# mLSTM cell and exact-GELU block on one Trainium2 core: the decays' turning split in two, and the front's steps in a new order

## Chip, cores and metric

The kernel runs on one core of one Trainium2 chip. The metric is the device time of one execution in microseconds (us), the median of several runs. The engines are TensorE (PE, with its weight loads as PEld), VectorE (DVE), ScalarE (ACT), GpSimd (POOL) and SyncE (SP), which issues all DMAs here.

## The reference

An mLSTM cell runs over a sequence, and its output goes through a block of two matrices with an exact GELU between them.

```
batch, heads, seq, head_dim = 4, 8, 768, 40
for t in range(seq):
    m_new = max(f[t] + m, i[t])
    f_stab, i_stab = exp(f[t] + m - m_new), exp(i[t] - m_new);  m = m_new
    C = f_stab * C + i_stab * outer(v[t], k[t])
    n = f_stab * n + i_stab * k[t]
    y[t] = sigmoid(o[t]) * (C @ q[t]) / max(|n . q[t]|, 1)
x = y as (3072 tokens, 320);  out = gelu(x @ w_in) @ w_out      # w_in 320 x 2048, w_out 2048 x 320
```

Everything is float32; the two weight matrices arrive as float64, and the kernel converts their bits itself.

## The kernel before

**Chunks.** The sequence is cut into six chunks of 128 steps. Within a chunk the cell is a masked product of 128 by 128 per head (queries by keys, times weights that come from the gates), and a state of 40 by 41 per head carries over to the next chunk. A unit of work is one chunk c of one batch entry b: eight heads. A chunk of all four entries makes 512 tokens, which then go through the GELU block.

**The front.** The program first does the cell for chunks 0 and 1 and the whole GELU block for chunk 0, mixed with the conversion of all 26 weight pieces. This stage is the front. It takes up the first 133 us of the profiled execution. After it, the function `up` and the string DOWN handle each further chunk in the same way; neither is touched.

**The order is written by hand.** The string FRONT is a list of words. `play` goes through it and calls one step for each word; the letter names the step and the digits are its arguments. Every step issues its instructions on the engines' queues at once, and each engine works through its queue in that order, waiting for its inputs and for free buffers. So the place of a word sets the place of all its instructions on PE, DVE, ACT, POOL and SP. DMAs are issued by SP, also in order, and each waits until the one eight places before it has landed.

The steps that the texts speak of (small letters for chunk 0, capitals for chunk 1, the digit is the batch entry):

- `E`, `N` (`second_gates`, `later_gates`): the gate scans on DVE, the write of M to DRAM (`M_d`), the turns of `a` on PE into `aT`, and the exponentials of `ew` and `gg` on ACT. For chunk 0 they run ahead of the list.
- `Q`, `D` (`decays_turned`, L242): turn `ew` and `gg` on PE (L216), copy them to `ewT` and `gT` on DVE (L217), then spread the last row of `gT` over all partitions with a product (`pd`, L246) and copy it to `dec` (L248). Q is for the later chunks, D for the first.
- `w`/`W` (`weights`): for chunk 0, five-part products on PE into two PSUM banks `pm` (L394, L396), then eight exponentials on ACT (L399); for chunk 1 the input is a row broadcast from `M_d` by a DMA (`B`, L160), masked on POOL (`M`, L373).
- `t`/`T` (`turn`): keys and queries turned on PE (`pt`, L442), copied as `kT`, `qT` by ACT (L445). `s`/`S` (`scores`): 16 passes on PE (`ps`, L468) and two products with the weights on DVE (L471).
- `c`/`C` (`carry`): the state's products (`pf`, L487, L492); for chunk 0 it first weighs the values on DVE (`vw`, L455). `v`/`V` (`values`): `ph`, L531.
- `g`, `y`, `x`: the output gate's sigmoid on ACT (L405); the finishing on DVE (L544 to L549) with a small copy `y_rest` (L555); the turn to tokens (`px`, L566). For chunk 1 `X` is followed by `R` (`split_x`).
- `P`, `L`, `O`, `B`: DMAs only (weight pieces; q and k; v and output gate; the broadcast of `M_d`). `L0` and `O0` belong to batch entry 0 of chunk 0, `L4` and `O4` to entry 0 of chunk 1.
- `K`, `J` (`conv_one`, `conv_two`): the next weight piece's two conversion steps: three DVE instructions and two on ACT, then two on DVE (L337, L340) and the DMA of the piece four places on.
- `A`, `U`: up steps (`pu`, L671, L677, then GELU on ACT, L681) for the two halves of chunk 0's tokens. `F`: one row of the down product (`po`, L779). `Z`: one weight tile split in two parts.
- `k` (`warm`, L198): n products that nobody reads ("cold"). `I` (`keep_clock`): as many unread products (L354) ahead of the next step that allows for them.

Each word of the kind K, J, A, U, F or Z takes the next item of its own list, so only its place matters.

Of the kernel before, what the change touches and what calls it, by code (L numbers as in the profile page):

```python
# [25 lines left out]


FRONT = """
    k3 O0 L0 g0 I2 I2 E P0 w0 t0 P1 L1 k5 N k1 O2 P2 L3 L2 w1 K Q D s0 O1 t1 w2 c0 P3 K v0 I1 J K s1 y0 I4 I3 w3 t2
    I6 O3 v1 g1 L4 J I2 c1 I2 I3 K y1 s2 x0 t3 O4 B5 x1 J L5 B4 s3 v2 g3 g2 c2 v3 y2 T0 H G0 c3 K J x2 O6 y3 O5 A x3  # L30
    J M1 K K J M0 W0 L6 A J M2 W1 S0 C0 T1 K J U U K K T2 V0 A O7 J W2 G1 K M3 J K S1 C1 G2 Y0 L7 A W3 S2 V1 J J Y1
    C2 K T3 J K U U J S3 V2 K C3 K J K J J F K F F J F K X0 J G3 K J K V3 F F F J R0 K Y2 Z J F K K F J F K X1 J F R1
    F J K F X2 F B8 F Y3 J Z X3 R2 B9 R3 B10 F"""
DOWN = """
    M0 Z M1 W0 F L3 F W1 Z Z F S0 Z S1 K2 C0 M2 Z C1 G0 G1 G2 G3 V0 Z V1 W2 Z M3 F Q2 K3 Q3 Y0 D3 F F W3 F Z S2 S3
    C2 C3 V2 V3 F N F Y1 X0 R0 Y2 F F Y3 X1 R1 F X2 R2 F X3 R3 F"""
# [3 lines left out]
def kernel(  # L40
# [18 lines left out]
    B, H, S, D = q.shape  # L59
    L = P  # L60
    NCH = S // L
# [67 lines left out]
    def load(n, first=0, end=4):  # L129

        if n >= NCH * B:
            return
        c, b = divmod(n, B)
        for src, dst in ((q, qb), (k, kb), (v, vb), (o_gate, None))[first:end]:
            nc.sync.dma_start(out=dst[turn_of(n)][:, :, 0:D] if dst else out_of(n),
                              in_=src[b, :, c * L:(c + 1) * L, :].rearrange("h p d -> p h d"))
# [73 lines left out]
    def gates_turned(*parts):  # L210

        for src, dst in parts:
            n = dst.shape[1]
            pg = ps_tr.tile([P, n, BH], F32, name="pg", tag="tr")
            for c in range(n):
                nc.tensor.transpose(pg[:, c, :], src[:, c, :], ident[0:BH, 0:BH])  # L216
            nc.vector.tensor_copy(out=dst, in_=pg)  # L217
# [24 lines left out]
    def decays_turned(e0, e1, g0, g1):  # L242
        e, g = slice(e0, e1), slice(g0, g1)
        gates_turned((ew[:, e], ewT[:, e]), (gg[:, g], gT[:, g]))
        pd = ps_tr.tile([P, g1 - g0, BH], F32, name="pd", tag="tr")
        nc.tensor.matmul(pd.rearrange("p c n -> p (c n)"), last, gT[:, g].rearrange("p c n -> p (c n)"),  # L246
                         start=True, stop=True)
        nc.vector.tensor_copy(out=dec[:, g], in_=pd)  # L248
# [65 lines left out]
    def conv_one(i):  # L314

        if i < len(pieces):
            n = bits[i].shape[1]
            lo, hi = bits[i][:, :, 0], bits[i][:, :, 1]
            s = sig[i] = raw.tile([P, WP], F32, name="sig", tag="sig")[:, 0:n]
            p = pow2[i] = raw.tile([P, WP], F32, name="pow", tag="pow")[:, 0:n]  # L320
            su, pu = s.bitcast(U32), p.bitcast(U32)

            nc.vector.tensor_scalar(out=pu, in0=hi, scalar1=20, scalar2=0x7FF,
                                    op0=OP.logical_shift_right, op1=OP.bitwise_and)
            nc.scalar.activation(out=p, in_=pu, func=AF.Relu, scale=-I23, bias=e_hi)
            nc.scalar.activation(out=pu, in_=p, func=AF.Relu, scale=-1.0, bias=e_lo)

            nc.vector.tensor_scalar(out=su, in0=hi, scalar1=0xFFFFF, scalar2=0x100000,
                                    op0=OP.bitwise_and, op1=OP.bitwise_or)
            nc.vector.scalar_tensor_tensor(out=s, in0=lo, scalar=2.0 ** -32, in1=su, op0=OP.mult, op1=OP.add)  # L330

    def conv_two(i):

        if i < len(pieces):
            hi, p = bits.pop(i)[:, :, 1], pow2.pop(i)
            pu = p.bitcast(U32)
            nc.vector.scalar_tensor_tensor(out=pu, in0=hi, scalar=0x80000000, in1=pu,  # L337
                                           op0=OP.bitwise_and, op1=OP.bitwise_or)
            dst, s = pieces[i][1], sig.pop(i)
            nc.vector.scalar_tensor_tensor(out=dst, in0=s, scalar=2.0 ** -20, in1=p, op0=OP.mult, op1=OP.mult)  # L340
            fetch(i + NB)
# [343 lines left out]
    def first_up_steps(h):  # L685

        def step(k):
            ups.append((len(ups) + len(tags_next) % 2, (2 * k, 2 * k + 2, HT * h, HT * h + HT)))
            if len(ups) == 2:
                first_up()  # L690

        return [lambda k=k: step(k) for k in range(HF // 2)]

    def first_up():
        if len(ups) == 1:
            tags_next.append(1)
        if ups:
            up_step(first_g, ups)
        ups.clear()
# [68 lines left out]
    def send(c, b, o_sb):  # L768
        nc.sync.dma_start(out=out[b * S + c * L:b * S + (c + 1) * L, :], in_=o_sb)

    def first_down_steps(g):
        po = []

        def row(f):

            if f == 0:
                po.extend(ps_mm.tile([P, DM], F32, name="po", tag="ab"[b // 2]) for b in range(B))
            for b in range(B):
                nc.tensor.matmul(po[b], g.t[:, f, b * L:(b + 1) * L], w_out[:, f, :], start=(f == 0),  # L779
                                 stop=(f == NF - 1))  # L780
                if f == NF - 1:
                    if b % 2 == 0:
                        o_sb = outp.tile([P, 2, DM], F32, name="o_sb", tag="o_sb")
                    nc.scalar.copy(out=o_sb[:, b % 2, :], in_=po[b])
                    send(0, b, o_sb[:, b % 2, :])

        return [lambda f=f: row(f) for f in range(NF)]

    def down_steps(c, g):
        A = lambda e, h: lambda j, t: g.t[:, HF * e + j, HT * h + t * L:HT * h + (t + 1) * L]  # L790
        Sm = lambda s: lambda j, t: s[j // (HF // 2)][:, j % (HF // 2), t * L:(t + 1) * L]
# [53 lines left out]
        def p4(pb, tiles=slice(0, 2)):  # L845
            add(block(1, 0)[:, tiles], pb, block(1, 0)[:, tiles])
            for t in range(2)[tiles]:
                send(c, 2 + t, o_sb[1][:, t, :])

        todo = ((A(0, 0), Bm[0][0], 0, True, p1), (Sm(g.s2), T[2], 1, True, p6),  # L850
                (A(1, 0), Bm[1][0], 0, False, p2), (Sm(g.s1), T[1], 2, True, p5),
                (A(0, 1), T[3], 3, True, p7), (A(1, 0), Bm[1][1], 2, False, p3),
                (A(1, 1), T[4], 3, False, p4))
# [9 lines left out]
    def in_turn(steps):  # L863
        todo = list(steps)
        return lambda: todo.pop(0)() if todo else None

    def cell_steps(c, letters, before=None):
# [7 lines left out]
    n_pieces = range(len(pieces))  # L875
    steps = dict(P=fetch, L=lambda n: load(n, 0, 2), O=lambda n: load(n, 2, 4), B=load_M, E=second_gates, N=later_gates,
                 I=keep_clock, k=warm, D=lambda: decays_turned(0, 2, 0, 1), Q=lambda: decays_turned(2, NCH - 1, 1, NCH - 1),
                 A=in_turn(first_up_steps(0)), U=in_turn(first_up_steps(1)), F=in_turn(first_down_steps(first_g)),
                 K=in_turn(lambda i=i: conv_one(i) for i in n_pieces), H=products_begin,
                 J=in_turn(lambda i=i: conv_two(i) for i in n_pieces), Z=split_weight)  # L880
    steps |= cell_steps(0, "mwgtscvyx") | cell_steps(1, "MWGTSCVYXR")
    play(FRONT, steps)
    for c in range(1, NCH):
        g, later, steps = Hidden(True), [], {}
# [38 lines left out]
```

## Time and profile before

| | us |
|---|---|
| median of 4 runs | 488.65 (488.33 to 489.0) |
| profiled execution | 489.87 |
| its span | 488.10 |
| PE busy | 477.4 (98%) |
| DVE busy | 348.6 (71%) |
| ACT busy | 222.6 (46%) |
| POOL busy | 70.5 (14%) |
| front ends (first product of `up`) | 133.19 |

The profile is one execution. "Busy" counts an engine's instructions, and PE's products overlap, so a busy PE may still run slowly. In the views, times are us from the start of the span; in square brackets stands the idle time of the engine just before an instruction and what released it.

### The profile page before, as it was taken

The numbers are of one execution on the slowest core, as the hardware profiler recorded it, in microseconds if no ns is written. First come the engines' busy times: TensorE is split into PE (matmuls) and PEld (weight loads), VectorE is DVE, ScalarE is ACT, GpSimd is POOL, SyncE is SP. The second block draws the span as 40 slices with busy tenths as digits, with TensorE's granted clock in tenths as the row PEclk, the third lists the DMA queues.
The fourth block names the chain that finished last, engine by engine and source line by source line (L and its number), as shares of the span: only waits on it lengthen the run. The fifth ranks groups of instructions, "written<-read, shape, count | busy, mean of one in ns | idle before, by whom it ended". The sixth has DMA issues, their size and how long they took to land.

```text
span 488.1 us, 10810 instructions
## 1 busy us (share of the span) xinstructions
PE 477.4 (98%) x4224; PEld 417.4 (86%) x4224; DVE 348.6 (71%) x728; ACT 222.6 (46%) x477; POOL 70.5 (14%) x108
## 2 busy tenths in 40 slices
PE   8898999999999999999999999999999999999997
PEld 8687888877777899977899977899977899977996
DVE  7689878889979998867397857398857387724321
ACT  7595999854533852203861203862203762211300
POOL 3002020000110127200144200126000112000000
PEclk9799999999999999999999999999999999999999
DMA  6997964255851355921365831256931350100001
GB/s 147 184 215 212 221 141 100 89 140 131 143 136 13 37 95 96 215 45 20 34 127 78 179 65 20 32 88 102 192 71 19 34 90 3 37 19 0 1 1 54
DMA packets 164434, 44.24 MB, mean 91 GB/s; under 512 B 154176, under 2 KB 157408, under 8 KB 164384
## 3 DMA queue, kind: packets, MB, share of 16 engines
q1 hardware_dynamic: 164384, 43.56, 45.3%
q8 instruction: 33, 0.54, 0.5%
q14 instruction: 17, 0.14, 0.1%
HBM read 39.52 MB, written 4.01 MB: 89 GB/s over the span
## 4 chain that ended last, share of the span: by engine, by line
PE 83%; DVE 10%; ACT 3%; DMA 2%; issue 1%; DVEq 0%; SPq 0%
PE po L802 26%; PE pu L726 21%; PE po L779 7%; PE pu L671 6%; PE pu L737 6%; PE ps L468 4%; PE ph L531 4%; PE pf L492 2%; PE pf L487 2%; DVE g L832 2%; PE pu L677 2%; DMA W<-M_d 1%; DVE ob L549 1%; PE px L566 1%; PE pt L442 1%
## 5 line engine op out<-in xcount | busy, mean ns | idle before, releaser
L802 PE MATMUL po<-w_out,g 128*128 128x160 f32 x640 | 91.2, 300 | 0.0
L741 ACT ACTIVATE g<-pu 128x512 f32<-128x512 f32 x80 | 40.8, 614 | 108.1 <-PE pu L737 108.0
L802 PEld LDWEIGHTS po<-w_out,g 128*128 128x128 f32 x640 | 87.8, 190 | 1.8 <-ACT g L741 1.8
L399 ACT ACTIVATE W<-W,aT 128x128 f32<-128x128 f32 x160 | 48.9, 389 | 3.1 <-POOL W L373 3.0
L802 PE MATMUL po<-w_sums,sums 128*128 128x160 f32 x320 | 47.2, 302 | 0.0
L802 PEld LDWEIGHTS po<-w_sums,sums 128*128 128x128 f32 x320 | 44.2, 190 | 0.4
L576 ACT ACTIVATE x_hi<-px 128x384 fp32r<-128x384 f32 x20 | 9.8, 489 | 74.1 <-PE px L566 74.1
L471 DVE TENSOR_TENSOR W<-ps,W 128x512 f32<-128x512 f32 x48 | 30.3, 684 | 16.0 <-ACT W L399 9.3
L726 PE MATMUL pu<-x_hi,w_in_hi 128*128 128x512 f32 x160 | 41.4, 400 | 0.0
L726 PE MATMUL pu<-x_lo,w_in_lo 128*128 128x512 f32 x160 | 40.6, 396 | 0.0
L658 DVE TENSOR_TENSOR sums<-g 128x512 f32<-128x512 f32 x20 | 13.8, 689 | 33.3 <-ACT g L741 33.3
L373 POOL TENSOR_SCALAR_AFFINE_SELECT W<-W 128x1024 f32<-128x1024 f32 x20 | 23.3, 1168 | 98.4 <-DMA W<-M_d 98.1
L726 PEld LDWEIGHTS pu<-x_hi,w_in_hi 128*128 128x128 f32 x160 | 29.4, 188 | 8.2 <-ACT g L741 1.9
L726 PEld LDWEIGHTS pu<-x_lo,w_in_lo 128*128 128x128 f32 x160 | 30.1, 188 | 7.2
L779 PE MATMUL po<-w_out,g 128*128 128x320 f32 x128 | 35.5, 434 | 0.0
L815 DVE TENSOR_TENSOR o_sb<-po,o_sb 128x320 f32<-128x320 f32 (+1 forms) x27 | 12.5, 464 | 27.4 <-PE po L802 23.5
L779 PEld LDWEIGHTS po<-w_out,g 128*128 128x128 f32 x128 | 23.9, 190 | 9.5
L726 PE MATMUL pu<-x_all,w_in_mid 128*128 128x512 f32 x80 | 31.7, 396 | 0.1
L726 PE MATMUL pu<-x_all,w_mid 128*128 128x512 f32 x80 | 31.7, 396 | 0.0
L630 DVE TENSOR_TENSOR w_in_mid<-w_in_hi,w_in_lo 128x512 fp32r<-128x512 f32 x20 | 14.7, 733 | 21.6 <-PE pu L726 21.6
L671 PE MATMUL pu<-first_x,w_in 128*128 128x256 f32 x128 | 29.0, 382 | 0.3 <-DVE W L471 0.3
L411 POOL MEMSET g<- 32x1024 f32 x8 | 7.6, 945 | 146.9 <-ACT W L399 146.6
(169 smaller groups left out, 891.3 us busy)
## 6 DMA issues: line engine op xcount, KB each, us to landing
W<-M_d SPq DMA_DIRECT2D x20, 512.0 KB, 5.5
bits<-in_moe_w_in_dram SPq DMA_DIRECT2D x20, 256.0 KB, 4.3
bits<-in_moe_w_out_dram SPq DMA_DIRECT2D x16, 320.0 KB, 3.1
ob<-in_o_gate_dram SPq DMA_DIRECT2D x24, 160.0 KB, 3.6
out_dram<-o_sb SPq DMA_DIRECT2D x24, 160.0 KB, 2.1
vb<-in_v_dram SPq DMA_DIRECT2D x22, 160.0 KB, 5.1
kb<-in_k_dram SPq DMA_DIRECT2D x22, 160.0 KB, 4.8
blocks<-in_k_dram SPq DMA_DIRECT2D x48, 32.0 KB, 2.2
```

The lines of the kernel that those rows point to most:

```text
L373: nc.gpsimd.affine_select(out=t, in_=t, compare_op=OP.is_ge, fill=1.0e30, base=0, pattern=[[0, H], [1, L]], channel_multiplier=-1)
L399: nc.scalar.activation(out=W[n][:, h, :], in_=src, func=AF.Exp, scale=-1.0, bias=aT[:, self.c, r:r + 1])
L468: nc.tensor.matmul(ps[hip][:, p, :], kT[r, p, :], qT[r, p, :], start=True, stop=True)
L471: nc.vector.tensor_tensor(out=w, in0=ps[hip], in1=w, op=OP.mult)
L531: nc.tensor.matmul(ph[r, h, :], Pm[:, h, r], vb[turn_of(n)][:, h, :], start=True, stop=True)
L630: nc.vector.tensor_tensor(out=w_mid[i], in0=w_hi[i], in1=w_lo[i], op=OP.add)
L671: nc.tensor.matmul(banks[-1][e][:, i - i0, :], in_tile(i, x)[:, e, i % 2 * P:(i % 2 + 1) * P], first_x[:, x, t0:t1], start=(x == 0 and i = ...
L726: nc.tensor.matmul(pus[i][e], w[k][:, e, i * P:(i + 1) * P], x[:, k, :], start=(n == 0 and k == 0), stop=False, skip_group_check=True)
L737: nc.tensor.matmul(pu[e], w[r, i // 2, i % 2 * P:(i % 2 + 1) * P], x[r, NX, :], start=False, stop=(n == 2), skip_group_check=True)
L741: nc.scalar.activation(out=g.t[:, HF * e + i, :], in_=pu[e], func=AF.Gelu, scale=4097.0)
L779: nc.tensor.matmul(po[b], g.t[:, f, b * L:(b + 1) * L], w_out[:, f, :], start=(f == 0), stop=(f == NF - 1))
L802: nc.tensor.matmul(bank[at][:, i, :], lhs(j, t), rhs(j), start=(first and i == 0 and j == 0), stop=(i == n - 1 and j == HF - 1), skip_grou ...
```

## The change

`decays_turned` loses its second half, which becomes a step of its own, `decays_last`: the product that spreads the last row of `gT` and the copy of it. Two new letters call it, `q` for the later chunks and `d` for the first. The words of FRONT stand in a new order: 191 words instead of 192. Every step of the old list occurs in the new one as often as before, except for `I` (six instead of nine, with other counts) and `k` (three in both, with other counts). In the changed kernel all lines behind L244 stand three lines lower.

```
 FRONT = """
-    k3 O0 L0 g0 I2 I2 E P0 w0 t0 P1 L1 k5 N k1 O2 P2 L3 L2 w1 K Q D s0 O1 t1 w2 c0 P3 K v0 I1 J K s1 y0 I4 I3 w3 t2
-    I6 O3 v1 g1 L4 J I2 c1 I2 I3 K y1 s2 x0 t3 O4 B5 x1 J L5 B4 s3 v2 g3 g2 c2 v3 y2 T0 H G0 c3 K J x2 O6 y3 O5 A x3
-    J M1 K K J M0 W0 L6 A J M2 W1 S0 C0 T1 K J U U K K T2 V0 A O7 J W2 G1 K M3 J K S1 C1 G2 Y0 L7 A W3 S2 V1 J J Y1
-    C2 K T3 J K U U J S3 V2 K C3 K J K J J F K F F J F K X0 J G3 K J K V3 F F F J R0 K Y2 Z J F K K F J F K X1 J F R1
-    F J K F X2 F B8 F Y3 J Z X3 R2 B9 R3 B10 F"""
+    I2 O0 g0 L0 P0 L1 E k1 t0 P1 P2 k7 w0 N w1 O1 K L2 Q s0 O3 w2 q D d k2 P3 t1 w3 c0 L3 J v0 t2 K K y0 s1 I7 v1 I8
+    O2 J g1 L4 I5 c1 K I1 I2 y1 s2 x0 t3 B4 O4 B5 g2 J x1 s3 v2 c2 L5 y2 H T0 x2 G0 v3 g3 c3 K y3 M1 J L6 J A x3 M0 K
+    W0 O7 K A O6 O5 J M2 W1 S0 C0 K J J T1 U U K L7 V0 K T2 J J A G2 K G1 Y0 W2 S1 K M3 C1 A J S2 J K W3 K V1 C2 Y1
+    T3 J J U U S3 V2 K K J G3 J Y2 C3 X0 K V3 J K F J F K K B8 F J K F F J K F F F R0 X1 J J K F J F K X2 F J K F J
+    Y3 Z F R1 F K J B9 B10 F X3 R2 Z R3 F"""
...
     def decays_turned(e0, e1, g0, g1):
         e, g = slice(e0, e1), slice(g0, g1)
         gates_turned((ew[:, e], ewT[:, e]), (gg[:, g], gT[:, g]))
+
+    def decays_last(g0, g1):
+        g = slice(g0, g1)
         pd = ps_tr.tile([P, g1 - g0, BH], F32, name="pd", tag="tr")
         nc.tensor.matmul(pd.rearrange("p c n -> p (c n)"), last, gT[:, g].rearrange("p c n -> p (c n)"),
                          start=True, stop=True)
...
+                 d=lambda: decays_last(0, 1), q=lambda: decays_last(1, NCH - 1),
```

Among the moves: `t0` stands ahead of `w0`; `s0` and `w2` stand between `Q` and `q`, and `D`, `d` and two cold products follow; `P0` and `L1` stand ahead of `E`, `P1` and `P2` between `t0` and `w0`; `B4` stands ahead of `O4`; `X0` and `V3` stand ahead of the first `F`; the last `Z` stands between `R2` and `R3`.

## The prediction

> **What bounds the kernel now.** I read the page first. Its sections 1 and 2:
>
> ```profile
> PE 477.4 (98%) x4224; PEld 417.4 (86%) x4224; DVE 348.6 (71%) x728; ACT 222.6 (46%) x477; POOL 70.5 (14%) x108
> ...
> PEclk9799999999999999999999999999999999999999
> ```
>
> TensorE (PE) is busy nearly always, and its clock was below full in one slice only, the second (12.2 to 24.4 us). Next the chain that ended last, in order of time (start, us, what):
>
> ```profile
> 15.67 0.78 PE pd L246 x2
> 17.43 0.63 PE pd L246 x2
> 18.06 2.01 PE ps L468 x16
> 20.07 1.90 PE pt L442 x8
> ...
> 57.38 7.17 PE pu L671 x32
> ```
>
> Up to 15.67 the chain is DVE's gate work. From 15.67 to 22.4 it is PE at half speed: 16 score passes took 2.01 here, and 0.89 at 53.97. From 22.8 to 57 it changes between ACT, DVE, a DMA and PE; from 57.38 to the front's end at 133.19 it is all PE. The busy times by stretch say the same (columns: PE, PEld, DVE, ACT, POOL busy, granted clock, DMA share, GB/s):
>
> ```profile
> 12.30:15.71 3.41, 1.42 (x14) 0.86 (x12) 3.28 (x9) 2.35 (x8) 0.00 (x0) 1.00 1.34 201
> 15.71:22.54 6.83, 6.51 (x36) 5.46 (x37) 3.27 (x9) 3.26 (x8) 0.00 (x0) 0.50 0.97 177
> 36.19:39.61 3.42, 2.53 (x49) 2.10 (x49) 2.89 (x6) 1.60 (x5) 0.00 (x0) 1.00 0.69 194
> 20.17:49.56 29.39, 27.59 (x360) 23.61 (x360) 26.96 (x60) 22.44 (x51) 2.54 (x2) 0.96 0.88 201
> 57.38:133.19 75.81, 75.81 (x573) 59.98 (x574) 65.86 (x165) 55.32 (x103) 7.06 (x7) 1.00 0.57 129
> ```
>
> The first window was 42% busy and half speed followed for 6.83 us; the third was 74% busy and nothing followed. From 20.17 to 49.56 DVE is nearly full (its idle time is 0.86 and 0.50; the rest is gaps between instructions), and PE's many products there are partly unread ones. In the last stretch PE has no hole, while DVE has 9.9 us and ACT 20 us of slack. The timeline shows how the middle begins and ends:
>
> ```profile
> 20.17 1.29 DVE L471 TENSOR_TENSOR W<-ps,W 128x512 f32<-128x512 f32 x2 [1.88 <-PE ps L468]
> ...
> 21.15 0.59 ACT L445 COPY kT<-pt 128x512 f32<-128x512 f32 x1 [3.27 <-PE pt L442]
> ...
> 41.65 1.39 DVE L455 TENSOR_TENSOR vw<-v,ewT 128x328 f32<-128x328 f32 x1
> ...
> 49.61 2.89 PEld L671 LDWEIGHTS pu<-first_x,w_in 128*128 128x128 f32 x14 [0.25 <-DVE w_in L340]
> ```
>
> DVE and ACT both stood still for the slow PE; DVE's conversion of the fifth weight piece (J, done at 49.56) then released PE's second up step. So the time of the first product with the scores on DVE (20.17) is carried through DVE's row to PE.
>
> **The change, part by part.** By the order of instructions on each engine, nothing but places changes: 22 cold products instead of 21, 16 unread ones instead of 17, all else equal in number; behind the front the order is the same.
>
> *Up to 15 us.* t0 now stands ahead of w0, with seven cold products between. PE: t0 from 7.75 (after the turns of aT, which ran at 7.00) to 8.6, the cold ones to 10.1 (14 passes of 0.107), w0 to 11.0 (0.87 as at 11.83), aT's turns to 11.4, w1 in two halves as ACT frees its banks, to 13.3. ACT: kT and qT 8.6 to 9.7, then W0 (2.1) from 10.7 to 12.8. DVE's gate chain does not move: its subtraction ends at 13.24 and ACT's exponentials start at 13.28, as before, 0.4 after W0. Gain and loss nothing, if t0's data are there.
>
> *15 to 20 us.* Behind Q's turns (end 15.0) PE no longer waits for gT but has s0 at once: 0.89, so DVE's product starts at 16.1 instead of 20.17, 4.1 earlier. w2 follows as ACT frees banks (16.95), then q, D, d: each waits for a DVE copy, but that wait now stands behind s0 and w2. Queued behind them is t1: it ends at 19.6, and ACT, busy with W1, the first conversion and W2, asks for it at 20.0. The 3.27 of idle ACT is gone.
>
> *The clock.* It decides whether 16.1 holds. Window 12.30 to 15.71 would hold half of w1 0.45, turns 0.37 and 0.43, s0 0.71: 1.96 of 3.41, or 57%, between the rows that fell (42%) and held (74%). I take "holds" as slightly likelier. If it falls, s0 ends 0.2 later, and d and t1 0.7 (one window) to 1.3 (two): 0.7 to 1.3 on DVE's row. The Trainium skill (TensorE: Matmul & The Clock Gate, Part 1) says that half speed comes after an idle window of some 3.4 us. The trace's 6.83 is two such windows, but PE was not idle ahead of it, so the measurement decides; by the rule the clock would hold and the sum be the one without the 0.7.
>
> *20 to 50 us.* DVE's instructions from the first score product to J of the fifth piece are the same set, plus the four copies of ewT, gT and dec (0.29, 0.23, 0.19, 0.19) that now lie inside. Before: 29.39 less 1.36 idle is 28.0. After: 16.1 + 28.0 + 0.9 + 0.5 of waiting for d is 45.5, 4.0 ahead. I checked who else could be late: L2, O1 and L3 follow from the DMA rate in the rows (201, 177 GB/s) by 18, 17 and 24, wanted at 22, 27 and 31; s3 and the sigmoid of ob_118 come within 0.2 of DVE's need, so new idle is 0 to 1.5. The two masks on POOL made DVE's vw 1.39 instead of 0.49 and a y_rest 0.93 instead of 0.23; both stay in the sum, though they could fall on nothing (up to 1.6 less).
>
> SP: P0 and L1 go ahead of M_d's write, P1 and P2 behind it; B4 ahead of O4. M_d's broadcast then starts at about 30 instead of 35.3, and its mask, W0 on ACT, is not wanted until 48.
>
> *PE at the U steps.* J ends at 45.5; the second up step ended 4.34 behind it (53.90), now 49.9; scores, carry and turn took 3.0: 52.9. Before, PE was let go at 57.38 by the product of S0. That needs W0 on ACT: the first up step starts 1.1 behind vw of c3 (43.04 before; 16.1 + 21.5 + 1.4 = 39.0 now), so at 40.1 at most, ends 4.7 later, and W0 7.75 later less one conversion pair (1.43): 51.1. PE's own 52.9 is the later. Gain 57.38 - 52.9 = 4.5; I take 4.4.
>
> *To the front's end.* PE's order there has the same work (V3 and X0 now ahead of the first F), without holes before, so the 4.4 go through. DVE has one J more left (1.4) against 9.9 of slack. V3 loses the four F steps (8.7 us) that covered it; DVE's product for S3 should end 1.2 ahead of it. At the end Z and R3 leave DVE some 1.3 us later against PE than before, but PE reads the joined weights only two thirds into the 11.16 of the next pair. Both at nothing; up to 2 if wrong.
>
> **The sum.** 4.4 off the profiled execution, 489.87 (its span 488.10 and 1.77 around it), is 485.5; that run is 1.2 above the median of 488.65. On the median's scale: 484.3.
>
> **Rivals.** *The clock falls all the same* (the change doesn't do what it says): 4.4 less 0.7 to 1.3: 485.0 to 485.6. For it: 57% is untested. Against it: the half-speed window would be full and so end after one.
>
> *The gain is given back later.* DVE waits newly between 20 and 45 (1.5), or V3 or the last splits wait (2): 1 to 3.4 left, 485.3 to 487.6. For it: DVE's row is tight in four places. Against it: 9.9 of slack behind 57.
>
> *Slower: t0's data.* t0 now heads PE's queue, and w0, aT's turns (hence DVE's later copies) and Q stand behind it. Its L0 (two loads of 160 KB as listed) is followed by P0 and L1, 0.85 MB, where the engines before fell idle from 6.8 to 8. If the engines share evenly, L0 lands with all 1.7 MB at 200 GB/s, near 10.6: 2.5 us on ACT's exponentials; PE's hole also closes the gate at 12.30, for 6.83 us at half speed, about 2.6 more. That is 5.1 against 4.4: 489.3. It decides from a landing of some 10 us. Against it: L0 was in by 6.8. The skill (DMA: Bandwidth & Descriptors, Queues, rings and completion order) has each engine take a queue's descriptors in ring order; then P0 costs L0 nothing. No row here shows two such loads overtaking each other.
>
> **How the numbers follow.** Forecast, 483.5 to 485.0: 0.50. Clock falls: 0.17. Given back: 0.16. More than forecast (no mask in DVE's way, 483.5 down to 482.7): 0.04. No change: 0.05. Slower: 0.08. The range takes all to 487.4 and leaves out some 0.17. What this kernel's measurement can tell is about 0.2%, 1 us; faster 0.86, same 0.05, slower 0.09.
>
> **What would show it.** Right: full clock from 15 to 23; the first score product on DVE near 16.1; the fifth J done near 45.5; the first pair of U steps near 53; the front's end near 128.8. Wrong: t0 waiting for a DMA behind 8.2, half speed, the J later than 47, or holes in PE between 53 and 128 (V3 above all).

## Result and the profile after

| | before | changed |
|---|---|---|
| median us (lowest to highest, executions) | 488.39 (486.87 to 489.48, 73) | 485.92 (483.97 to 491.09, 54) |
| profiled execution | 489.87 | 485.71 |
| first pair of U steps starts on PE | 57.38 | 53.08 |
| front ends (first product of `up`) | 132.78 | 129.81 |
| profiled time less the front's end | 357.1 | 355.9 |

The ratio is 0.996, with a 95% interval of 0.9952 to 0.9969. The change makes the kernel faster by about 2 us (by the ratio) to 2.5 us (by the medians). The forecast was 4.4. The front's end is read here from the timeline, as the start of the first product of `up`; by the chain of work it is 133.19 before (the number ahead of the prediction) and 130.22 now, where 128.8 was forecast.

A part of the changed kernel's spread has a plain reason: its executions differ in the granted clock. In 34 of 54 the mean clock was 0.998 or more, and their median is 485.56 (483.97 to 487.10). In 15 it was 0.995 or 0.996 (median 486.96), in 5 it was 0.990 to 0.993 (median 490.3). The kernel before had 0.988 to 0.993 in each of the 79 executions that ran beside the experiments. The profile of the changed kernel is one with full clock. Its page, PE's busy time and its granted clock by slices:

```profile
PE 474.5 (98%) x4224; PEld 415.8 (86%) x4224; DVE 346.4 (72%) x728; ACT 222.3 (46%) x477; POOL 70.0 (14%) x108
...
PEclk9999999999999999999999999999999999999999
```

The second slice shows full clock where before it showed 7. The chain that ended last, at the places that answer to those of before (start, us, what):

```profile
15.48 1.14 PE ps L471 x16
...
19.72 0.87 PE pt L445 x8
...
53.25 6.91 PE pu L674 x32
...
127.25 0.50 DVE w_out L343
127.80 2.42 PE po L782 x8
130.22 5.81 PE pu L729 x25
```

The score passes now stand right behind Q's turns and take 1.14 instead of 2.01, and the first pair of U steps starts 4.1 to 4.3 earlier. New is DVE ahead of 127.80: in the kernel before the chain was all PE from 57.38 to the front's end. The busy times by stretch (columns as before) say the same:

```profile
12.30:15.71 3.41, 2.23 (x21) 1.47 (x22) 3.31 (x10) 3.17 (x12) 0.00 (x0) 1.00 1.06 231
15.71:22.54 6.83, 6.40 (x94) 5.30 (x91) 5.52 (x16) 6.80 (x24) 0.00 (x0) 1.00 1.04 170
53.25:129.81 76.56, 75.22 (x572) 59.47 (x572) 67.22 (x162) 55.05 (x103) 8.49 (x8) 1.00 0.64 148
89.40:127.74 38.34, 37.06 (x228) 26.86 (x226) 34.69 (x88) 18.68 (x35) 4.13 (x4) 1.00 0.65 151
```

The window that was 42% busy is now 65% busy, and in this execution full clock follows. From the U steps to the front's end PE has 1.34 of hole that it did not have before. In the last stretch, from DVE's product for S3 to its last conversion, DVE is busy 34.69 of 38.34 and POOL 4.13; the same stretch of the kernel before had:

```profile
93.93:130.01 36.08, 36.08 (x224) 26.28 (x223) 32.77 (x88) 18.73 (x35) 1.48 (x2) 1.00 0.61 136
```

The number of DVE instructions is the same (88), but they take 1.9 longer, and the stretch 2.3. The timeline of the changed kernel shows where:

```profile
16.67 1.29 DVE L474 TENSOR_TENSOR W<-ps,W 128x512 f32<-128x512 f32 x2 [0.58 <-PE ps L471]
...
45.04 0.69 DVE L343 SCALAR_TENSOR_TENSOR w_in<-sig,pow 128x512 f32<-128x512 f32 x1
...
114.40 1.35 POOL L376 TENSOR_SCALAR_AFFINE_SELECT W<-W 128x1024 f32<-128x1024 f32 x1
...
114.84 1.26 DVE L343 SCALAR_TENSOR_TENSOR w_out<-sig,pow 128x320 f32<-128x320 f32 x1
...
122.62 1.17 POOL L376 TENSOR_SCALAR_AFFINE_SELECT W<-W 128x1024 f32<-128x1024 f32 x1 [6.87 <-DMA W<-M_d]
...
122.76 1.58 DVE L627 SCALAR_TENSOR_TENSOR w_in_lo<-w_in_hi,w_in 128x512 fp32r<-128x512 f32 x1
...
127.80 2.42 PE L782 MATMUL po<-w_out,g 128*128 128x320 f32 x8 [1.34 <-DVE w_out L343]
```

The first score product is at 16.67 (20.17 before), the fifth J ends at 45.73 (49.56 before). At 114.84 and 122.76 two DVE instructions that otherwise take 0.49 and 0.69 take 1.26 and 1.58, each while a mask runs on POOL. And the last F waits 1.34 for the last conversion.

### The profile page after: what moved, and what is told of

It is laid out like the page before. It is cut to its first block, busy times and chain, and to the rows that moved or that the text cites. A ratio compares the mean times of both kernels' runs of the same rounds, so it can differ in the third digit from the quotient of the medians.

```text
span 483.9 us, 10808 instructions
## 1 busy us (share of the span) xinstructions
PE 474.5 (98%) x4224; PEld 415.8 (86%) x4224; DVE 346.4 (72%) x728; ACT 222.3 (46%) x477; POOL 70.0 (14%) x108
## 4 chain that ended last, share of the span: by engine, by line
PE 80%; DVE 11%; ACT 3%; SPq 2%; issue 1%; DMA 1%; POOL 1%; DVEq 0%; POOLq 0%
PE po L805 30%; PE pu L729 21%; PE pu L674 6%; PE pu L740 6%; PE ps L471 4%; PE ph L534 4%; PE pf L495 2%; PE pf L490 2%; PE pu L680 2%; SPq L145 2%; DVE w_out L343 1%; PE px L569 1%; PE pt L445 1%; DVE pow L340 1%; DVE W L474 1%
## 5 line engine op out<-in xcount | busy, mean ns | idle before, releaser
L729 PEld LDWEIGHTS pu<-x_hi,w_in_hi 128*128 128x128 f32 x160 | 29.4, 188 | 8.2 <-ACT g L744 1.8
```

What stands on the lines that cost most here:

```text
L729: nc.tensor.matmul(pus[i][e], w[k][:, e, i * P:(i + 1) * P], x[:, k, :], start=(n == 0 and k == 0), stop=False, skip_group_check=True)
```

## Experiments

The theory after the first reading (A): the head gains its 4 us; 1.2 to 1.3 are given back at the last F, and the clock, which still falls in some executions, takes the rest. Rivals: the clock has no part; the gain is all clock; the order around the split makes it. All times are medians with lowest, highest and number of executions; "U" is the start of the first pair of U steps on PE, "front" the front's end, both of the profiled execution.

| kernel | us | ratio, interval | U | front |
|---|---|---|---|---|
| after_filled | 485.09 (484.57 to 485.85, 6) | 0.9927 [0.9911, 0.9943] | 53.03 | 129.07 |
| before_filled | 487.45 (485.30 to 488.66, 12) | 0.9968 [0.9953, 0.9984] | 56.56 | 131.97 |
| split_only | 488.01 (487.56 to 489.30, 12) | 0.9990 [0.9979, 1.0001] | 57.27 | 132.67 |
| after_last_conv | 486.91 (485.09 to 491.80, 12) | 0.9976 [0.9948, 1.0004] | 58.05 | 134.50 |
| old_full_clock | 487.20 (486.02 to 487.60, 10) | 0.9974 [0.9965, 0.9983] | 54.99 | 130.40 |
| split_full_clock | 487.30 (486.05 to 488.94, 11) | 0.9980 [0.9969, 0.9991] | 56.25 | 131.66 |
| filled_old_tail | 484.27 (484.25 to 484.44, 4) | 0.9919 [0.9906, 0.9931] | 53.00 | 128.33 |
| filled_k_early | 484.60 (483.58 to 486.62, 6) | 0.9929 [0.9910, 0.9948] | 54.98 | 130.50 |
| filled_b4_late | 485.66 (485.10 to 486.52, 6) | 0.9941 [0.9928, 0.9953] | 53.68 | 130.24 |
| split_full_b4_early | 486.67 (486.06 to 488.70, 11) | 0.9966 [0.9953, 0.9979] | 55.96 | 131.36 |
| filled_split_undone | 487.21 (485.81 to 488.31, 11) | 0.9974 [0.9963, 0.9985] | 54.56 | 131.19 |
| filled_t0_back | 486.36 (486.07 to 487.44, 6) | 0.9958 [0.9945, 0.9971] | 53.81 | 130.47 |
| filled_b8_late | 484.76 (484.54 to 485.63, 5) | 0.9922 [0.9909, 0.9936] | 53.33 | 129.02 |

The profiled times of these 13 kernels lie 355.3 to 356.5 behind their fronts' ends, so the front's end tells the time.

**The clock in the changed kernel: after_filled.**

```
-    k7 w0 N w1 O1 K L2 Q s0
+    k7 w0 N k3 w1 O1 k2 K L2 Q s0
```

> The changed kernel with five more cold products, three ahead of w1 and two behind it, where PE had holes of 0.43 and 0.43 us between 12 and 14 us. Theory A (the head gains its 4 us; the shortfall against the forecast is 1.2 to 1.3 us that the last F gives back by waiting for the last conversion on DVE, and about 0.5 us in the median from executions in which the clock still falls in the head): the granted clock is full, the median falls from 485.9 to 485.2 to 485.5, and the runs above 487 disappear. Rival B (the clock has no part in the spread or the shortfall): 485.9 with the same spread. Rival C (the cold products delay Q's turns and so DVE's first score product by up to 0.3): up to 486.2.

The clock was 0.998 or more in all six executions, and none was above 485.85. Four of the kernels below have the same head (filled_old_tail, filled_k_early, filled_b4_late, filled_b8_late); with them it is 27 executions, and none of them lost a window. The window of before and the last F (window, then timeline):

```profile
12.30:15.71 3.41, 3.20 (x31) 2.61 (x32) 3.31 (x10) 3.16 (x11) 0.00 (x0) 1.00 0.97 230
```
```profile
127.06 2.42 PE L782 MATMUL po<-w_out,g 128*128 128x320 f32 x8 [0.64 <-DVE w_out L343]
```

So five products that nobody reads are worth 0.8 by the medians, of which 0.36 is what the falls did to the median (485.92 against 485.56 at full clock); the other 0.5 is not clear of the scatter. The first score product stayed at 16.66, so C is out. The U steps did not move either. The wait of the last F is 0.64 here instead of 1.34: in this profile no mask fell on the Z.

**The clock in the old order: before_filled.**

```
-    L3 L2 w1 K Q D s0
+    L3 L2 w1 k7 K Q D s0
```

> The kernel before with seven cold products behind w1, in the hole of 0.97 us ahead of Q's turns; the order is the old one. It asks how much of the change is the clock. Theory A: full clock at 15.7 to 22.5 us, the first score product on DVE near 18.2 instead of 20.17, so 2 us less at the U steps and 486.4 to 487.0, depending on how much of it DVE's chain to the last conversion gives back. Rival B (the clock's fall is hidden, or not to be had by filling): 488.4. Rival D (the whole gain of the change is the clock): 485.9.

Six executions kept the clock (median 486.31), six lost one window (median 488.00). The profiled one lost one:

```profile
15.14:18.55 3.41, 2.31 (x25) 1.82 (x24) 1.80 (x7) 3.19 (x10) 0.00 (x0) 1.00 0.81 128
18.55:21.96 3.41, 3.41 (x24) 2.84 (x21) 2.44 (x6) 1.17 (x2) 0.00 (x0) 0.50 1.08 234
```

By this run the old order at full clock would stand near 486.3, and the clock is a large part of the change's gain, but not all of it. The first score product was late all the same (19.48), and the fall is not removed, since the window from 15.14 is still only 68% busy.

**The split alone: split_only.**

```
-    w1 K Q D s0 O1 t1
+    w1 K Q s0 q D d O1 t1
```

> The kernel before with the split alone: s0 stands between Q's turns and the spreading of the last row (Q s0 q D d), all other words in the old order. Theory A (the place of s0 makes the head's gain): the first score product on DVE at 16.2 to 16.9, kT of entry 1 about 3 us earlier, U steps 3 to 4 us earlier, and with the old tail less is given back than in the changed kernel: 485.0 to 485.9. Rival E (the order around it makes the gain: t0 ahead of w0, w2 ahead of q, the cold products): 487.3 to 488.4. Rival B' (the clock falls as before and eats it): the first product at 16.7 but t1 near 20, 486.5 to 487.

The first score product came at 16.67, as in the changed kernel, and it gained nearly nothing: 488.01. A window that was 64% busy was followed by half speed from 16.87 to 23.69, and PE, not DVE, was then late for the second score product (windows, then timeline):

```profile
13.46:16.87 3.41, 2.19 (x25) 1.85 (x25) 2.80 (x8) 3.03 (x10) 0.00 (x0) 1.00 1.34 181
16.87:20.28 3.41, 2.25 (x12) 1.94 (x11) 2.41 (x8) 1.46 (x3) 0.00 (x0) 0.50 0.98 207
```
```profile
26.35 1.29 DVE L474 TENSOR_TENSOR W<-ps,W 128x512 f32<-128x512 f32 x2 [2.01 <-PE ps L471]
```

Of theory A's numbers only the first product was right. B' and E both stay possible from this run.

**The last conversion ahead of Z and R1: after_last_conv.**

```
-    F J Y3 Z F R1 F K J B9 B10 F X3
+    F J K Y3 F J Z F R1 B9 B10 F X3
```

> The changed kernel with the last K ahead of Y3 and the last J behind it, ahead of the Z and R1 that stood before it on DVE (F J K Y3 F J Z F R1 B9 B10 F). Theory A (the last F waits 1.34 us for the last conversion, and that is what the front gives back): no wait at the last F, the front ends 1.2 us earlier against the U steps, 484.6 to 484.9. Rival F (what DVE does last is only moved: Z, R1, R2 and R3 come 1.3 later and the first pairs of up wait for the parts): 485.7 to 486.0, with the wait at the products of L729 or behind. Rival G (the loss is not there but elsewhere): 485.9.

The six executions at full clock have a median of 485.50, the changed kernel's have 485.56: no gain, as F said, though the wait is not where F put it. The profiled execution was one of those that lost most clock (490.53), so its times cannot be set against the others, but it shows two things. PE does not wait for the last conversion any more, but ahead of it for a `px` bank that R1 frees:

```profile
132.23 0.41 PE L569 MATMUL px<-ident,ob 128*128 128x128 f32 x2 [1.20 <-DVE x_all L588]
```

And the clock fell at 14.77, after a window that was 71% busy, and stayed at half until 25.00, three windows:

```profile
11.36:14.77 3.41, 2.41 (x23) 1.39 (x20) 3.27 (x10) 3.10 (x10) 0.00 (x0) 1.00 0.99 260
14.77:18.18 3.41, 3.12 (x25) 2.84 (x26) 1.68 (x5) 3.38 (x11) 0.00 (x0) 0.50 1.10 179
```

**The old order at full clock, without and with the split: old_full_clock, split_full_clock.** These and the following run without falls, so that only the order differs.

```
-    w1 K Q D s0 O1 t1
+    w1 k7 K Q k5 q D k2 d s0 O1 t1        (old_full_clock)
+    w1 k7 K Q s0 k1 q D k2 d k2 O1 t1     (split_full_clock)
```

> The kernel before in its old order, with 14 more cold products in PE's holes between 13 and 17 us (seven behind w1, five behind Q's turns, two ahead of the spreading for the first chunk); s0 stays behind D. It keeps the clock at full speed and gives the change's order nothing. Theory H (most of the measured gain is the clock, which the old order loses for two windows in every execution): all runs at full clock, the first score product on DVE at 17.7 to 18.2, 485.9 to 486.5, that is 2.0 to 2.6 of the kernel before's 488.5. Rival I (the order carries it, the clock is a side matter): 487.3 or more.

> The old order with the split alone (Q s0 q D d), and cold products in the holes beside it (seven behind w1, one behind s0, two ahead of and two behind the spreading for the first chunk). Theory H: without the cold products the split gained 0.5 since the clock fell one window later and PE was late for the second score product instead; with full clock the first product is at 16.7, the second no longer waits 2.0 for PE, and the time is 485.0 to 485.8, 0.3 to 1.0 below the old order at full clock. Rival E (the broadcasts and loads of the old order hold the U steps whatever the clock does): 486.2 to 486.6, no better than the old order at full clock.

All 21 executions had a clock of 0.999 or more. The old order gained 1.2 (488.41 to 487.20), between H's 2.0 to 2.6 and rival I, and nearer to I; its first score product was at 19.61, where 17.7 to 18.2 was expected, since PE still turns and spreads ahead of s0. The cold products themselves take a share: the two copies of the spread row came at 17.04 and 18.45, and at 16.67 and 17.99 in before_filled, which has none there. With the split the first product is at 16.69 and the second waits 0.46 instead of 2.01, and yet the time is the same, 487.30. In that profile ScalarE's W0 waits for POOL's mask, and that for the broadcast of `M_d`; the U steps follow (POOL, ACT, PE in one timeline):

```profile
51.66 1.56 POOL L376 TENSOR_SCALAR_AFFINE_SELECT W<-W 128x1024 f32<-128x1024 f32 x1 [7.37 <-DMA W<-M_d]
...
53.26 2.45 ACT L402 ACTIVATE W<-W,aT 128x128 f32<-128x128 f32 x8 [0.30 <-POOL W L376]
...
56.25 3.94 PE L674 MATMUL pu<-first_x,w_in 128*128 128x256 f32 x17 [1.55 <-DVE W L474]
```

So in the old order the next thing that is late in this profile is a DMA. Rival E is right that the split alone is worth nothing there even at full clock (its own number, 486.2 to 486.6, was too low).

**The broadcast's place: filled_b4_late, split_full_b4_early.**

```
-    x0 t3 B4 O4 B5 g2 J x1 s3 v2 c2 L5 y2     (after_filled)
+    x0 t3 O4 B5 g2 J x1 s3 v2 c2 L5 B4 y2
-    t3 O4 B5 x1 J L5 B4 s3                    (split_full_clock)
+    t3 B4 O4 B5 x1 J L5 s3
```

> The changed kernel with the five cold products, and with B4, the broadcast that chunk 1's first weights need, back behind L5 as in the kernel before. Theory K (at full clock the old order is held by this broadcast: its mask ran at 50.14 and 51.66 in the two runs of the old order with full clock, and W0 on ScalarE and the U steps behind it): the mask ends after 50, W0 starts at 51 to 53, the U steps at 54.5 to 56, 486.2 to 487.5. Rival L (the broadcast has slack, as the prediction took it): U steps at 53.2, 485.1.

> The old order with the split, the cold products and one more word moved: B4 ahead of O4, as in the changed kernel. Theory K: the mask runs near 43, W0 no longer waits for it, the U steps start at 54 or before (56.25 without the move), 485.0 to 486.0 instead of 487.3. Rival L: 487.3. Rival M (all loads of the old order are late together, and another one takes the broadcast's place): 486.3 to 487.3, with a wait for another DMA.

In the new order the broadcast has slack: its mask ran at 44.43, not after 50, and W0 at 49.49. The cost is 0.6 by the medians, hardly more than the scatter, so K is out and L is nearer. Its last F waits 1.24, which is more than the 0.64 of after_filled. The profile shows what a later mask can do instead: it ran beside DVE's conversion for the second up step (1.46 for 0.69), and PE waited for that (POOL, DVE, PE):

```profile
44.43 1.36 POOL L376 TENSOR_SCALAR_AFFINE_SELECT W<-W 128x1024 f32<-128x1024 f32 x1 [3.75 <-DMA W<-M_d]
...
44.87 1.46 DVE L343 SCALAR_TENSOR_TENSOR w_in<-sig,pow 128x512 f32<-128x512 f32 x1
...
46.38 3.29 PE L674 MATMUL pu<-first_x,w_in 128*128 128x256 f32 x14 [0.59 <-DVE w_in L343]
```

In the old order the earlier broadcast gave 0.6 (487.30 to 486.67), less than K asks (1.3 or more) and hardly clear of the scatter. W0 no longer waits for the mask, but DVE now waits for other loads of the old order:

```profile
29.89 0.43 DVE L326 TENSOR_SCALAR pow<-bits 128x512 uint32<-128x512 uint32 x1 [0.82 <-DMA bits<-in_moe_w_in_dram]
...
40.71 0.50 DVE L458 TENSOR_TENSOR vw<-vb,ewT 128x328 f32<-128x328 f32 x1 [1.24 <-DMA vb<-in_v_dram]
```

That is M: the loads are late together. It points to the new order of the DMA words as what lets the earlier head through; no run moved these words alone, so this is argued and not shown.

**One part of the new order undone: filled_split_undone, filled_t0_back.**

```
-    Q s0 O3 w2 q D d k2 P3 t1
+    Q k5 q D k2 d s0 O3 w2 P3 t1     (filled_split_undone)
-    E k1 t0 P1 P2 k7 w0 N
+    E k1 P1 P2 k7 w0 t0 N            (filled_t0_back)
```

> The changed kernel with the five cold products, and the split undone: the spreading of both chunks stands ahead of s0 and w2 again, with cold products in its holes (Q k5 q D k2 d s0 O3 w2). Theory N (the split is worth the time that s0 comes earlier on DVE, as far as PE and the broadcast let it through): the first score product at 18.0 to 19.6 instead of 16.7, U steps 1 to 2.5 later than 53.2, 486.0 to 487.5. Rival O (the slack of DVE's row hides it, so the split has no part in the gain once the clock holds): 485.1.

> The changed kernel with the five cold products, and t0 back behind w0. The prediction says that t0's place ahead of w0 changes nothing: 485.1, s0 at 15.4 as before. Rival P (t0 ahead of w0 keeps PE busy in the first windows or frees ScalarE for W0): s0 later by 0.3 to 1, or the clock falls, 485.5 to 487.

Without the split the first score product is at 19.62, the U steps are 1.5 later than in after_filled, and the time is 487.21, 2.1 more. With t0 behind w0 it is at 17.60, since aT's turns wait for ScalarE's copy of kT, and the time is 486.36, 1.3 more:

```profile
13.24 0.43 PE L216 MATMUL pg<-ident,a 32*128 32x32 f32 x4 [1.43 <-ACT kT L448]
```

N and P hold by the times; the first product without the split was as late as N allowed at most. In both profiles the last F also waits longer (1.25 and 1.12, against 0.64 in after_filled), so about 0.5 of each loss is DVE's second half. And the seven cold products that fill the holes ahead of s0 in filled_split_undone are a part of its delay (some 0.4 to 0.5, by the copies at 17.05 and 18.46 against before_filled's): 2.1 is the most that the split can be worth there.

**The second half: filled_old_tail, filled_k_early, filled_b8_late.** filled_old_tail is after_filled with the kernel before's words behind the first `U U` (without O7, which the new head already has). The others:

```
-    R0 X1 J J K F J F K X2 F J K F J Y3 Z F R1 F K J B9
+    R0 X1 J K J K F F J K X2 F J K F J Y3 Z F R1 F J B9     (filled_k_early)
-    K K B8 F      and   F K J B9 B10
+    K K F         and   F K J B8 B9 B10                     (filled_b8_late)
```

> The changed kernel with the five cold products, and with the kernel before's words behind the first pair of U steps. Theory A' (the new order of the front's second half gives back 0.6 to 1.3, since its last F waits for the last conversion on DVE): the U steps stay at 53.2, the front's end follows them by 75.4 as in the kernel before (75.9 in the run with the cold products, 76.7 in the changed kernel), 484.3 to 484.7. Rival J (DVE's old tail needs more cover than the earlier head leaves it): the old tail waits too, 485.1 or more, with holes ahead of V3 or the last F.

> The changed kernel with the five cold products, and the last four K each one step earlier (J K J K F F J K X2 F J K F J Y3 Z F R1 F J), so that ScalarE's pair lies beside another conversion on DVE. Theory A': DVE loses four waits of 0.46, the last conversion ends 1.3 to 1.8 earlier, the last F does not wait, 484.3 to 484.7. Rival F (what follows on DVE is the bound: Z, R1, R2, R3 and the joined weights): 485.0 to 485.2, with a wait at px or at the first products of up instead.

> The changed kernel with the five cold products, and B8, the first broadcast for chunk 2, back behind the last J (the kernel before has it five conversions later than the changed one). Theory Q (the last F waits because GpSimd's first mask for chunk 2 now falls into DVE's last stretch: a conversion at 115.00 took 1.26 instead of 0.49 while the mask ran, and in the changed kernel's own run also a Z at 122.76 took 1.58 instead of 0.68): the mask runs behind 127, the conversion takes 0.49, the last conversion ends 0.7 to 0.8 earlier and the last F no longer waits (0.64 in the run without the move); 484.3 to 484.6. Rival R (DVE's row is held by the order of its own instructions, the five waits of 0.46 for ScalarE and the Z and R1 ahead of the last J): the wait stays at 0.5 or more, 485.0 to 485.2.

With the old second half PE has no wait from the U steps on; the front ends 75.33 behind them (76.04 in after_filled, 76.73 in the changed kernel), and the time is 484.27. That is the best of all kernels here, 4 us below the kernel before, and beats the changed one. With the K steps earlier the last F still waits 0.19, the front ends 75.52 behind the U steps, and the best two executions are the shortest of all (483.58 and 483.59). The profiled one was the longest of the six, with its U steps at 54.98 behind a load of `vb` that took 5.96 (DVE waited 1.29 for it). With the broadcast of chunk 2 later (by the lists of words it is seven conversions later in the kernel before, not five), the conversion took 0.49 again, a small copy met the mask instead (0.93 for 0.23), and the wait fell to 0.36 (0.64 in after_filled). The median of 484.76 is not apart from after_filled's 485.09 by more than the scatter. The mask of B8 ran at 121.70, and not behind 127 as Q expected, since SP had sent off this broadcast and the next two from 116.77 on, ahead of DVE's last conversion (DVE, DVE, PE):

```profile
115.02 0.49 DVE L343 SCALAR_TENSOR_TENSOR w_out<-sig,pow 128x320 f32<-128x320 f32 x1
...
122.02 0.93 DVE L558 COPY y_rest<-ob 128x128 f32<-128x128 f32 x1
...
127.00 2.42 PE L782 MATMUL po<-w_out,g 128*128 128x320 f32 x8 [0.36 <-DVE w_out L343]
```

So the wait is a sum, and Q and R both have a part: POOL's masks in DVE's way, and DVE's own order with its waits for ScalarE and the Z and R1 ahead of the last conversion.

## Why the prediction was right and wrong

*Up to 15 us.* "Gain and loss nothing" was too simple. t0 ahead of w0 is worth 1.3 in the new order (filled_t0_back). The feared wait for t0's data did not come: its turns ran at 8.34 without a wait for a DMA, so the rival on the slow side has no ground. The gates' chain ran 0.48 later in the changed kernel's profile, and equally in four profiles of the old order (before_filled, split_only, old_full_clock, split_full_clock), so that is not the change; it is why the first score product was at 16.67 and not 16.1.

*15 to 50 us.* Right. The fifth J was forecast to end at 45.5 and ended at 45.73; the U steps were forecast for 52.9 and came at 53.08. Some luck is in it: the first score product was 0.57 later than forecast, and DVE's row from there to the fifth J took 29.06, where the sum has 29.4. The reason given was incomplete: the prediction took the masks and broadcasts as having slack. In the new order that is so (filled_b4_late: 0.6 at most); in the old one the same early s0 gained nothing (split_full_clock), and the broadcast and the loads came later there.

*The clock.* A smaller step failed here, the one that placed a single window at 12.30 and judged it between the rows of 42% and 74%. Half speed followed windows that were 42, 64, 68 and 71% busy, and it began at 15.71, 16.87, 18.55 and 14.77 in four executions. The stretches at half speed were 6.82, 6.82, 3.41 and 10.23, whole windows. Each ended with its first window in which PE was busy throughout (3.41 of 3.41); windows of 66% (split_only) and 91% (the kernel before, and two in after_last_conv) did not end it, so "the half-speed window would be full" held in before_filled alone. The Trainium skill (TensorE: Matmul & The Clock Gate, Part 1) says that the window runs freely, from no fixed point of the kernel; the four starts agree. It also says that half speed comes after an idle window, and there the runs decide otherwise: PE was up to 71% busy. In the changed kernel's profile the least busy 3.41 us, from 11.8 to 15.2, hold 2.12, or 62%; with five more cold products no stretch that starts between 8 and 21 us holds less than 2.98 (87%), and no fall was seen. But PE's busy share alone does not decide: in after_last_conv, on the grid of windows that its own fall shows, an earlier window was 57% busy, and full clock followed:

```profile
4.53:7.95 3.42, 1.96 (x16) 1.73 (x16) 3.17 (x11) 2.67 (x3) 0.77 (x3) 1.00 1.05 203
```

What else decides stays open. A fall cost 1.4 for one window and 4.7 in the median of the five executions that lost more, against 0.7 to 1.3 in the prediction, and it came in 20 of 54. "Holds" was the likelier case, and the median moved by 0.36 only.

*To the front's end.* This is the step that failed most, a term that was mis-sized: "Both at nothing; up to 2 if wrong". It measured 1.33. The 9.9 of DVE's slack was summed over the whole stretch from 57 to 133, but 6.6 of it lay ahead of the product for S3 (29.96 busy of 36.55), where it helps nobody at the end. That stretch of the kernel before:

```profile
57.38:93.93 36.55, 36.55 (x342) 31.36 (x342) 29.96 (x72) 34.83 (x66) 4.48 (x4) 1.00 0.54 126
```

In the changed kernel DVE waited 2.02 for the scores of S3 at 89.40 and then ran in one chain, with a wait of 0.46 for ScalarE in each of five conversions, to the last one at 127.74. That chain took 38.34, and PE reached the last F 1.34 earlier. In the kernel before it took 36.08, and PE did not wait. Of the 2.26 between them 1.66 is the two instructions that met POOL's masks (1.26 for 0.49, 1.58 for 0.69), and 0.3 is in the waits for ScalarE (2.3 against 2.0). The first of the masks is B8's, which stands seven conversions earlier; the second is B9's, issued at 116.13 instead of 131.40. The prediction named Z, R3 and V3 as what might be late, and left out B8 and B9, whose masks run on POOL. That the second half is the cause is shown by filled_old_tail, where the old words stand behind the same head and PE has no wait; how the 1.33 divides between masks and order is not settled (filled_b8_late). The Trainium skill (SBUF — State Buffer, Who interferes with whom) states that a VectorE instruction with two inputs in SBUF contends with a GpSimd instruction that reads SBUF; the rows at 114.84 and 122.76 are of that kind, at 2.6 and 2.3 times their usual duration.

*The sum.* From the profiles: 4.30 at the U steps (57.38 to 53.08), 1.33 given back (75.40 to 76.73), so 2.97 at the front's end. Executions at full clock stand 2.83 below the median of before; the falls take 0.36 of it. That makes 2.5. Of the 1.9 that the forecast had too much, 1.33 is the term put at nothing and 0.36 the clock; the rest, some 0.2, is not assigned. With the clock held and the old second half (filled_old_tail) the time is 484.27, and the forecast was 484.3. The scaling of the profiled execution to the median was right: behind the front it is 0.6 to 1.8 longer than the other profiles, and 1.2 had been taken off.

*The rivals.* "The gain is given back later" is what happened, in 485.3 to 487.6, by another wait than the two named. "The clock falls all the same" happened in a part of the executions. What the prediction did not see is how much of the kernel before's time was the clock itself: cold products alone give the old order 1.2 (old_full_clock) to 2.4 (the six executions of before_filled at full clock).

## What to carry to other kernels

Slack is not a sum: find the last instruction on which another engine waits for the engine that "has room", and follow that engine back from there; what lies behind its last wait is the slack that counts. When a word is moved, follow it to the end, through its DMA to the engine that it releases: here two broadcasts that stand earlier, one of them by seven conversions, put masks beside DVE's tightest stretch. And a hole in PE that costs nothing by itself can still cost a half-speed window, in some executions or in all; filling it with products that nobody reads was the cheapest gain here.

## What the runs showed of the hardware

- In four traces TensorE's clock fell after windows in which PE was 42 to 71% busy, at different times, and stayed at half for whole multiples of 3.41 us, until the end of a window in which PE was busy throughout. A window of 57% in one of them did not make it fall, so the busy share alone does not decide. The same program differs by up to 5 us between executions: 485.56 at full clock, some 490.6 in the four executions with a mean clock of 0.990, which is what three lost windows give in after_last_conv's profile.
- A mask on GpSimd stretched VectorE instructions that ran beside it: 0.49 to 1.26, 0.69 to 1.58, a copy from 0.23 to 0.93. Each ended only behind the end of the mask, by 0.1 to 0.6.
- Parts do not add up: the split is worth nothing in the old order (487.20 and 487.30) and up to 2.1 in the new one (487.21 and 485.09).
- Open: even at full clock the executions of most kernels here spread over 1 to 3 us (filled_old_tail's four over 0.2). One profile shows a load of `vb` of 5.96 ahead of late U steps; whether that is the rule was not tried.
